# New offsets on the sort keys that order the expert steps of an attention, mixture-of-experts and FFN kernel

## The chip, the cores and the metric

The kernel runs on one core of one Trainium2 chip. The metric is the device time of one execution in microseconds; the time of a kernel is the median of its runs. The core has five engines, each of which takes its instructions in the order in which they were written for it: TensorE (PE, matrix products; its weight loads are shown as PEld), VectorE (DVE), ScalarE (ACT), GpSimd (POOL) and SyncE (SP), which here only issues DMA transfers. ACT and POOL issue DMA transfers as well. Engines wait for each other by semaphores.

## The reference, cut to what matters

```python
attn_out = _attn_ref(q, k, v)            # 8 batches, 8 heads, 576 rows, 64 columns; linear attention
x = attn_out.transpose(0, 2, 1, 3).reshape(4608, 512)

logits = x @ w_gate                      # one of 8 experts for each token
e_idx = argmax(logits, axis=1)
gate_w = softmax(logits)[e_idx]
eom = 1.0 / (1.0 + exp(-(x @ w_output_gate)))
for e in range(8):
    mask = e_idx == e
    h = maximum(x[mask] @ w1[e], 0.0)    # 512 -> 1024
    out[mask] = gate_w[mask] * eom[mask, e] * (h @ w2[e])   # 1024 -> 512

h = out @ w_in                           # 512 -> 2048
return (h * cos(h)) @ w_out              # 2048 -> 512
```

All of it is float32, with 4608 tokens.

## The kernel before, in words

The kernel has three stages, which follow one another on PE: the attention with the gate (0 to 183 us of the span), the expert steps (183 to 661 us), and the FFN (its first products start at 669 us and run to the end).

A float32 product is made of three products in the fast matrix type: each operand is split into a high part and a remainder (`wh` and `wl` for weights, `xTh` and `xTl` for tokens, `hh` and `hl` for the hidden layer), and high by high, high by remainder and remainder by high are added in PSUM. The three products are L1141, L1143 and L1144 for the first expert layer (`mm1`, 128x256 outputs) and L1177 to L1179 for the second (`mm2`, 128x512 outputs).

**The expert steps.** After the tokens are sorted by expert, 22 steps j = 0 to 21 each take a block of tokens of one expert. Their kinds are D F D F D F H D F H F D F H D F H D F H F F: F is a step of 256 tokens (two tiles of 128), D is also one of 256 but shares its expert's weights with the step behind it, and H is a step of 128 tokens, one tile. The first two steps use tokens that are known early; those from j = 2 on need the sort. A step does this, for a tile a = 0, 1:

- POOL gathers the token rows by an indirect DMA (`gather`, L277) into one of two `xg` buffers and scales them (`norm`, L282); PE transposes them (`trans`, L287), ACT and DVE split them (`xhigh` L294, `xlow` L299). The names of these operations in the order are gat, norm, tr, xh and xl, and they are for a later step while the current one runs.
- SP loads a quarter of the expert's weights as they are (`wload`, L256, named ld; 1 MB each, three `raw` buffers); ACT rounds it in two halves (`whigh`, L264, named wh), DVE makes the remainder (`wlow`, L268, named wl). There is one set of wh/wl buffers for each of the four quarters, so a quarter is only split after the last product that reads the old one. Loads are numbered over the run: 4 for each change of expert weights.
- PE computes the first layer in four blocks n (named mm0 and mm1, the two halves of a block: a block has 24 products in an F or D step and 16 in an H step). In an H step the high and the remainder part of the tokens stand side by side, and ACT and DVE first add the two halves of the result (`hsum`, L1152/L1153, named hs). ACT takes the relu (`hhigh`, L1162, hh), DVE the remainder (`hlow`, L1166, hl). The block buffers in PSUM are three.
- PE computes the second layer (`mm2`); ACT copies the result out of PSUM (`yout`, L1183, named y) and issues its store on its own DMA queue (L1185).

**The sort** (operations named s: cnt, px, base, pos, hot, low, mm_0 to mm_2, inv, exp, eI, more, far, gate, done) runs beside steps 0 and 1. `mm_0` to `mm_2` are 36 small products of PE (L978); `inv` gives the row numbers that the gathers from step 2 on need.

**The conversion.** The FFN's weights come as 64-bit numbers. Beside the expert steps, 32 jobs load them (`c_load`, L1058, SP's queue, named cld; 'i' for the jobs of w_in, 'o' for those of w_out), and ACT, DVE and POOL turn them into float32 (csq L1063, clf L1066, ca L1071, ch L1075, cp L1079, cm L1082, cs L1086, cw L1099). Jobs 'o' store the result to memory from ACT's queue (chi, L1104). From the jobs 'i', sums and differences of blocks are made (wsum L1114 on POOL), split (whi L1122, wlo L1126) and stored (wst, L1129, ACT's queue), seven parts each time. Rows of the output that no token has are zeroed from ACT's queue too (zero, L1191).

At the end (Z operations): the first rows of the FFN's input are gathered (L1202), scaled (L1205), transposed (L1210) and copied (L1216), summed and split (xs L844, oh L852, ol L857).

**What sets the order.** Each operation is registered by `op(key, name, fn, *deps)`: `key` is a due time in a plan in which an F step is 21.6 long, a D step 21.4 and an H step 12.06 (L1190 to L1230 hold the tables). The plan's step starts are 43.6 for j = 2, 65 for j = 3 and 129.6 for j = 6. The table `SHIFT` (L1418 to L1451) adds an offset to the key, for each kind of operation and place; the place (`place`, from L1453 on) is for instance the kind of step (D, F, H, or the number for j = 0 to 2) and the tile, block or quarter. For gat, norm, tr, xh and xl, and for ld, wh and wl, the kind is that of the step before the one that they are for. Then `issue` (L24 to L56) writes the operations out: of all whose dependencies are written, always the one with the smallest key. An offset changes only the order; the operations, their engines and their buffers stay.

Of the kernel before, what the change touches and what calls it, by code (L numbers as in the profile page):

```python
# [56 lines left out]
def kernel(  # L57
# [14 lines left out]
    B, H, S, D = q.shape  # L72
# [38 lines left out]
    xs = dram.tile([N, XW], F32, name="xs")  # L111
# [125 lines left out]
    wh, wl, rawt, ereg = {}, {}, {}, [None]  # L237
# [64 lines left out]
    with ExitStack() as actx:  # L302
# [386 lines left out]
        for b in range(B):  # L689
# [45 lines left out]
            for c in range(C):  # L735
                i = C * b + c
# [7 lines left out]
            if b % 2:  # L744
                i = NM + b // 2
# [113 lines left out]
    with bctx:  # L859
# [229 lines left out]
        wf, wsum, wst = {}, {}, {}  # L1089
# [324 lines left out]
        for i, (at, e1, e2) in enumerate(ZO):  # L1414
# [4 lines left out]
            chi={('o',): 12.7},  # L1419
            cld={('i',): -3.65, ('o',): -18.9},  # L1420
            cm={('i',): 11.5, ('o',): 10.7},
            cp={('o',): 3.4},
            csq={('i',): 1.55, ('o',): 1.9},
            cw={('i',): 3.15, ('o',): 7.6},
            gat={('2', 1): 10.85, ('D', 0): -15.4, ('H', 1): 9.1},
            hh={('0', 2): 7.8, ('1', 2): -3, ('1', 3): -36.3, ('D', 0): 0.4, ('D', 1): 4.2, ('F', 2): -72.8, ('F', 3): -45.95,
                ('H', 3): -1.05},
            hl={('1', 1): 3.05, ('1', 3): -14.1, ('D', 2): 6.4, ('F', 2): -33.3, ('F', 3): -88.65, ('H', 3): -72.1},
# [3 lines left out]
            oh={(3,): 3.6, (4,): 25.85, (5,): 18.6},  # L1432
# [3 lines left out]
            wh={('1', 0, 0): -1.8, ('1', 2, 1): 5.25, ('F', 2, 0): -20.4, ('F', 2, 1): -0.95, ('F', 3, 0): 1.1, ('F', 3, 1):  # L1436
                0.85, ('H', 0, 0): -111.6, ('H', 0, 1): -36.8, ('H', 2, 0): -0.15, ('H', 2, 1): -3.4, ('w3', 0): -45.2, ('w3',
                1): -18.25},
            whi={(1,): 18.9, (2,): 17.9, (5,): 17.65},
            wl={('1', 0, 0): 4.65, ('1', 1, 0): 4.25, ('1', 2, 0): 3.35, ('F', 2, 1): 2.45, ('H', 0, 0): -164.95, ('H', 1, 0):  # L1440
# [321 lines left out]
```

## Time and profile before

| | us |
|---|---|
| median of three runs | 1454.03 |
| the three runs | 1454.03, 1456.35, 1449.67 |
| the profiled execution | 1452.48 |
| its span, first to last instruction | 1450.7 |
| mean granted clock of PE in it | 0.987 of full speed |

The span is what the profile's views divide up; the profiled execution's own time has the 1.8 us around it as well. A wait in a list of waits is idle time of the engine named first, up to the instruction given; the releaser is what ended it, inferred from semaphores. In a timeline, the idle time before an instruction stands in square brackets, and a line with xN stands for N neighbouring instructions. PEclk in a table of windows is the mean granted clock of PE, 1.00 being 2.4 GHz.

### The profile page before, as it was taken

The page shows a single profiled execution, that of the slowest core. Times are in us where ns is not written, and L with a number is a line of the kernel's source. Part 1 is how long each engine was busy: PE and PEld are TensorE (multiplying, and loading weights), DVE is VectorE, ACT ScalarE, POOL GpSimd, SP SyncE. Part 2 cuts the span into 40 slices and gives each one's busy share as a digit, 9 for nine tenths or more (in the row PEclk, how much of TensorE's full clock was granted, in tenths as well). Part 3 has the DMA queues.
Part 4 walks back from the last instruction along what each step waited for, and adds up shares of the span by engine and source line. Part 5 has one row for each costly group of instructions (what it writes and reads, how often), then busy time and mean ns, then how long its engine had stood idle before and what let it go on. Part 6 is the DMA issues. An engine that isn't in the chain of part 4 may idle for free.

```text
span 1450.7 us, 25366 instructions
## 1 busy us (share of the span) xinstructions
PE 1399.1 (96%) x9530; PEld 1247.3 (86%) x9530; DVE 970.9 (67%) x1465; ACT 871.9 (60%) x1613; POOL 545.9 (38%) x391
## 2 busy tenths in 40 slices
PE   6898899999999999998999999999999999999998
PEld 5777788898889889897889888898888898898987
DVE  7999986777877888876655655555565554655544
ACT  3876525546464746566766666666665666666654
POOL 5555325653536455425170513315041340603000
PEclk8999899999999999999999999999999999999999
DMA  9884434767896886996666665766667576665762
GB/s 312 274 266 157 173 103 169 269 234 260 286 356 223 284 268 239 342 334 240 189 203 195 203 199 172 226 175 205 197 181 224 167 209 197 197 203 169 206 178 82
DMA packets 189731, 317.99 MB, mean 219 GB/s; under 512 B 27744, under 2 KB 60000, under 8 KB 189600
## 3 DMA queue, kind: packets, MB, share of 16 engines
q1 hardware_dynamic: 153760, 253.54, 55.6%
q10 hardware_dynamic: 29840, 42.92, 8.0%
q0 software_dynamic: 6000, 19.83, 4.2%
q8 instruction: 78, 1.28, 0.4%
q14 instruction: 53, 0.43, 0.1%
HBM read 264.17 MB, written 52.05 MB: 218 GB/s over the span
## 4 chain that ended last, share of the span: by engine, by line
PE 78%; DVE 11%; DMA 4%; ACT 4%; issue 2%; POOL 0%; ACTq 0%; SPq 0%; DVEq 0%; POOLq 0%
PE acc L1629 8%; PE acc L1628 8%; PE acc L1627 8%; PE bank L1563 7%; PE bank L1565 7%; PE bank L1564 7%; PE hp L1141 5%; PE hp L1144 5%; PE hp L1143 4%; PE yps L1177 4%; PE yps L1178 4%; PE yps L1179 4%; DVE m L384 2%; DMA raw<-in_moe_w_dram 1%; PE xp L527 1%
## 5 line engine op out<-in xcount | busy, mean ns | idle before, releaser
L1563 PE MATMUL bank<-xo,wp 128*128 128x256 f32 x994 | 281.6, 283 | 1.4 <-ACT part L1577 0.6
L1564 PE MATMUL bank<-xo,wp 128*128 128x256 f32 x994 | 277.4, 279 | 0.9 <-DVE xo L857 0.9
L1565 PE MATMUL bank<-xo,wp 128*128 128x256 f32 x994 | 277.6, 279 | 0.0
L1606 DVE SCALAR_TENSOR_TENSOR n<-n,h 128x512 f32<-128x512 f32 x144 | 125.6, 872 | 171.0 <-ACT n L1603 171.0
L1627 PE MATMUL acc<-wh,ht 128*128 128x512 f32 x576 | 227.6, 395 | 0.4 <-ACT ht L1612 0.4
L1628 PE MATMUL acc<-wl,ht 128*128 128x512 f32 x576 | 227.5, 395 | 0.0
L1629 PE MATMUL acc<-wh,ht 128*128 128x512 f32 x576 | 227.0, 394 | 0.4 <-DVE ht L1616 0.4
L1563 PEld LDWEIGHTS bank<-xo,wp 128*128 128x128 f32 x994 | 186.9, 188 | 22.4 <-ACT part L1577 4.1
L1564 PEld LDWEIGHTS bank<-xo,wp 128*128 128x128 f32 x994 | 186.7, 188 | 17.3 <-DVE xo L857 1.1
L1141 PE MATMUL hp<-xTh,wh 128*128 128x256 f32 x704 | 193.7, 285 | 5.8 <-DVE ht L1166 5.3
L1144 PE MATMUL hp<-xTh,wl 128*128 128x256 f32 x704 | 192.1, 282 | 0.0
L1565 PEld LDWEIGHTS bank<-xo,wp 128*128 128x128 f32 x994 | 187.5, 189 | 0.0
L268 DVE TENSOR_TENSOR wl<-raw,wh 128x1024 fp32r<-128x1024 f32 x121 | 164.6, 1379 | 11.2 <-ACT wh L264 10.6
L857 POOL TENSOR_TENSOR xo<-x,xo 128x512 fp32r<-128x512 f32 x24 | 31.1, 1296 | 371.2 <-ACT xo L852 371.2
L1585 DVE TENSOR_TENSOR h<-bank,part 128x256 f32<-128x256 f32 x213 | 89.3, 421 | 110.9 <-PE bank L1565 109.8
L1143 PE MATMUL hp<-xTl,wh 128*128 128x256 f32 x544 | 152.8, 281 | 1.3 <-DVE xTl L299 1.3
L1592 ACT ACTIVATE n<-h 128x512 int32<-128x512 f32 x144 | 91.1, 633 | 101.7 <-DVE h L1585 98.1
L264 ACT CAST wh<-raw 128x1024 fp32r<-128x1024 f32 x126 | 127.8, 1053 | 38.0 <-DMA raw<-in_moe_w_dram 18.5
L1141 PEld LDWEIGHTS hp<-xTh,wh 128*128 128x128 f32 x704 | 134.7, 191 | 7.0 <-DVE ht L1166 5.7
L1600 ACT ACTIVATE n<-n 128x512 f32<-128x512 f32 x144 | 91.1, 633 | 77.9 <-DVE n L1597 77.9
L1144 PEld LDWEIGHTS hp<-xTh,wl 128*128 128x128 f32 x704 | 134.7, 191 | 0.2
L1629 PEld LDWEIGHTS acc<-wh,ht 128*128 128x128 f32 x576 | 108.3, 188 | 26.8 <-DVE ht L1616 1.7
(310 smaller groups left out, 3083.4 us busy)
## 6 DMA issues: line engine op xcount, KB each, us to landing
wp<-ws SPq DMA_DIRECT2D x504, 256.0 KB, 2.8
raw<-in_moe_w_dram SPq DMA_DIRECT2D x60, 1024.0 KB, 7.9
ws<-wst ACTq DMA_DIRECT2D x28, 512.0 KB, 7.2
ys<-yt ACTq DMA_DIRECT2D x39, 256.0 KB, 5.9
xs<-xt ACTq DMA_DIRECT2D x36, 260.0 KB, 4.2
k<-in_k_dram SPq DMA_DIRECT2D x8, 1024.0 KB, 8.3
v<-in_v_dram SPq DMA_DIRECT2D x8, 1024.0 KB, 8.7
q<-in_q_dram SPq DMA_DIRECT2D x8, 1024.0 KB, 9.3
```

The lines of the kernel that those rows point to most:

```text
L264: sc.copy(out=wh[j, c][:, s], in_=rawt[c][:, s])
L268: eng.tensor_tensor(out=wl[j, c][:, s], in0=rawt[c][:, s], in1=wh[j, c][:, s], op=ALU.subtract)
L1141: pe.matmul(hp[:, f2, :], w_h, xTh[j][:, d, :], start=(d == 0), stop=False)
L1143: pe.matmul(hp[:, f2, :], w_h, xTl[j][:, d, :], start=False, stop=False)
L1144: pe.matmul(hp[:, f2, :], w_l, xTh[j][:, d, :], start=False, stop=(d == KD - 1))
L1563: pe.matmul(h, w[:, 0, k], x[:, i, 0, k], start=(first and k == 0), stop=False, skip_group_check=True)
L1564: pe.matmul(h, w[:, 0, k], x[:, i, 1, k], start=False, stop=False, skip_group_check=True)
L1565: pe.matmul(h, w[:, 1, k], x[:, i, 0, k], start=False, stop=(k == 1), skip_group_check=True)
L1606: ve.scalar_tensor_tensor(out=rs[j, s], in0=rs[j, s], scalar=-0.5, in1=hs[j, s], op0=ALU.add, op1=ALU.mult)
L1627: pe.matmul(acc[t, a], gh[f][:, ts], w_h, start=(c == 0), stop=False)
L1628: pe.matmul(acc[t, a], gh[f][:, ts], w_l, start=False, stop=False)
L1629: pe.matmul(acc[t, a], gl[f][:, ts], w_h, start=False, stop=(c == KF - 1))
```

## The change

Only the table `SHIFT` is replaced. No operation is added, dropped or given to another engine. A place that the new table lacks has the offset 0. The change's own words are that the offsets come from a search that also counts the shared semaphores and the common bandwidth of the transfers. The diff, cut to the entries that are spoken of:

```diff
         SHIFT = dict(
-            cld={('i',): -3.65, ('o',): -18.9},
-            cm={('i',): 11.5, ('o',): 10.7},
-            gat={('2', 1): 10.85, ('D', 0): -15.4, ('H', 1): 9.1},
-            hs={('H', 0): -80.25, ('H', 1): -138.15, ('H', 2): -3.05, ('H', 3): -91.25},
-            ld={('F', 2): -13.65},
-            norm={('1', 0): -18.3, ('1', 1): 16.25, ('D', 0): -3.75, ('F', 0): -3.2, ('H', 0): 7.1},
-            s={('exp',): 14.15, ('gate',): 11.85, ('hot',): 15.45, ('mm_0',): 11.05, ('more',): 13.55, ('pos',): 16.35,
-                ('px',): 2},
-            tr={('D', 0): -68.85, ('F', 0): -1.55, ('H', 0): -100.5, ('H', 1): -76.35, ('Z', 2): 0.55},
...
-            wst={(0,): 33.95, (1,): 29.4, (2,): 22.8, (3,): 31.35, (5,): 29.6},
-            xs={(0,): 4.7, (3,): 3.85},
-            y={('0', 0): 7.35, ('1', 0): 10.15, ('D', 1): 12.45, ('F', 0): 1.5, ('F', 1): -47.1, ('H', 0): 11.6},
+            cld={('i',): -2.05, ('o',): 12.1},
+            cm={('i',): 13.2, ('o',): 14.1},
+            cs={('i',): -18},
+            gat={('1', 1): 9.15, ('2', 1): -17, ('H', 0): -23.3},
+            hs={('H', 0): -179.55, ('H', 1): -71.3, ('H', 2): -7.8, ('H', 3): -44.75},
+            ld={('F', 0): -5.65, ('F', 1): -6, ('H', 0): 7.95, ('H', 2): 15.25, ('H', 3): 18.1},
+            norm={('2', 0): -14.15, ('F', 0): 7.35, ('F', 1): 7.9, ('H', 0): 6.55, ('H', 1): 7.65},
+            s={('done',): 12.7, ('far',): -68.15, ('low',): 8.3, ('mm_0',): 13.75, ('more',): 0.95, ('pos',): 19.85, ('px',):
+                3.4},
+            tr={('1', 1): 1.85, ('2', 1): 0.55, ('D', 0): -3.5, ('F', 0): 3.95, ('H', 0): -51, ('H', 1): -114.7, ('Z', 2):
+                1.25},
...
+            wst={(0,): 14.85, (1,): 8.2, (2,): 11.45, (3,): 28.9, (4,): 41.55, (5,): 5.2, (6,): 10.35},
+            xs={(2,): 57.1},
+            y={('1', 0): 1.75, ('1', 1): 6.25, ('D', 0): 4.25, ('F', 1): 1.35, ('H', 0): 5.6},
```

The entries of chi, cp, csq, cw, hh, hl, oh, wh, whi, wl, wlo, wsum, xh, xl and zero are replaced too, and entries for ca, ch and ol come in.

## Rows read from the trace of the kernel before

**Rows 1.** The page, its span and the busy time of each engine.

```profile
span 1450.7 us, 25366 instructions
...
PE 1399.1 (96%) x9530; PEld 1247.3 (86%) x9530; DVE 970.9 (67%) x1465; ACT 871.9 (60%) x1613; POOL 545.9 (38%) x391
```

**Rows 2.** Windows by stage: us, busy by engine, PEclk, DMA share, GB/s.

```profile
183.00:661.00 478.00, 466.90 (x3071) 421.71 (x3071) 366.88 (x504) 259.29 (x399) 229.44 (x164) 0.99 0.74 261
661.00:690.00 29.00, 25.08 (x160) 21.42 (x161) 20.06 (x29) 18.07 (x37) 15.64 (x12) 1.00 0.64 218
```

**Rows 3.** Waits of PE, 183 to 690 us: us in total, times, longest.

```profile
PE hp L1141 <- DVE ht L1166: 5.3, 2, 3.0
PE t L287 <- POOL xg L282: 3.5, 3, 2.3
PE t L1210 <- POOL yg L1205: 1.5, 1, 1.5
PE hp L1143 <- DVE xTl L299: 1.3, 2, 1.0
```

**Rows 4.** Timeline of PE, at four of its waits: start, us, instruction, idle before.

```profile
231.56 0.66 PE L287 MATMUL t<-ident,xg 128*128 128x128 f32 x4 [0.67 <-POOL xg L282]
...
237.24 0.68 PE L287 MATMUL t<-ident,xg 128*128 128x128 f32 x4 [2.27 <-POOL xg L282]
...
339.60 0.38 PE L1141 MATMUL hp<-xTh,wh 128*128 128x256 f32 x1 [2.25 <-DVE ht L1166]
...
404.15 0.39 PE L1141 MATMUL hp<-xTh,wh 128*128 128x256 f32 x1 [3.01 <-DVE ht L1166]
```

**Rows 5.** Windows behind three waits, and two undisturbed first layers; columns as above.

```profile
237.30:241.00 3.70, 3.70 (x20) 3.70 (x21) 0.97 (x1) 0.00 (x0) 3.57 (x3) 0.56 0.00 0
339.60:343.00 3.40, 3.40 (x17) 3.40 (x18) 3.21 (x5) 2.32 (x5) 0.21 (x1) 0.58 1.04 372
404.20:408.00 3.80, 3.80 (x19) 3.61 (x20) 3.48 (x6) 2.95 (x6) 2.05 (x2) 0.60 0.96 337
308.20:319.30 11.10, 11.10 (x99) 11.05 (x99) 5.54 (x9) 4.04 (x6) 4.60 (x4) 1.00 0.70 260
349.10:360.50 11.40, 11.40 (x99) 11.40 (x98) 10.02 (x14) 7.83 (x13) 3.78 (x3) 1.00 0.27 94
```

**Rows 6.** Timeline of POOL from 218 us, and the tile xg from 217 to 236.

```profile
217.99 0.98 POOL L277 DMA_INDIRECT xg<-xs,invI  x1 [22.06 <-DVE es L1021]
220.60 1.31 POOL L1082 TENSOR_TENSOR rw<-rw,a 128x512 f32<-128x512 f32 x1 [1.62 <-ACT yt L1183]
...
223.81 2.13 POOL L282 TENSOR_TENSOR xg<-xg 128x512 f32<-128x512 f32 x1 [0.77 <-DMA xg<-xs,invI]
226.09 1.24 POOL L277 DMA_INDIRECT xg<-xs,invI  x1
...
236.09 1.10 POOL L282 TENSOR_TENSOR xg<-xg 128x512 f32<-128x512 f32 x1 [2.07 <-DMA xg<-xs,invI]
...
L287 PE MATMUL t<-ident,xg x8: 272/273/330, 227.5 to 231.9; 128*128 128x128 f32 x8
...
DMA to landing us min/median/max: 3.6/5.0/7.1
```

**Rows 7.** Timeline of PE, the products of the sort.

```profile
214.74 1.92 PE L978 MATMUL sp<-rpi,ht 128*128 128x108 bf16 x36
```

**Rows 8.** Timeline of ACT ahead of the H steps j = 6 and j = 9.

```profile
336.25 0.34 ACTq L1185 DMA_DIRECT2D ys<-yt  x1
336.63 0.37 ACT L1152 COPY ht<-hp 128x256 f32<-128x256 f32 x1 [5.07 <-DMA raw<-in_moe_w_dram]
...
397.14 0.59 ACT L1183 COPY yt<-yps 128x512 f32<-128x512 f32 x1 [5.40 <-DMA raw<-in_moe_w_dram]
```

**Rows 9.** Timeline of SP at 326 us, and how long that transfer took.

```profile
326.23 0.37 SPq L256 DMA_DIRECT2D raw<-in_moe_w_dram  x1
...
DMA to landing us min/median/max: 9.9/9.9/9.9
```

**Rows 10.** Waits of SP, 183 to 661 us: us in total, times, longest.

```profile
SPq L1058 <- DVE sq L1099: 65.9, 7, 15.2
```

More of the change, by code (lines that the diff above doesn't have):

```diff
@@ L1435 @@
-            tr={('D', 0): -68.85, ('F', 0): -1.55, ('H', 0): -100.5, ('H', 1): -76.35, ('Z', 2): 0.55},
[L1436 to L1440, printed above, removed]
-                -18, ('H', 1, 1): -7.45, ('H', 2, 0): -0.25, ('H', 3, 0): -1.25, ('w3', 0): -58.35},
@@ L1442 @@
[L1442 to L1449 removed]
+            ca={('o',): -6},
@@ new lines @@
+            ch={('o',): 5.4},
+            chi={('o',): 12.9},
+            cld={('i',): -2.05, ('o',): 12.1},
+            cm={('i',): 13.2, ('o',): 14.1},
+            cs={('i',): -18},
+            csq={('i',): 8.15},
+            cw={('i',): -24.4, ('o',): 10.55},
+            gat={('1', 1): 9.15, ('2', 1): -17, ('H', 0): -23.3},
+            hh={('D', 0): 7.35, ('D', 1): 3.75, ('D', 2): 7.8, ('D', 3): 5.75, ('F', 0): 2.7, ('F', 1): 2.65, ('F', 2): 2.5,
+                ('F', 3): -0.15, ('H', 0): 1.35},
@@ new lines @@
+            hl={('1', 0): 5.15, ('1', 1): 3.75},
+            hs={('H', 0): -179.55, ('H', 1): -71.3, ('H', 2): -7.8, ('H', 3): -44.75},
+            ld={('F', 0): -5.65, ('F', 1): -6, ('H', 0): 7.95, ('H', 2): 15.25, ('H', 3): 18.1},
+            norm={('2', 0): -14.15, ('F', 0): 7.35, ('F', 1): 7.9, ('H', 0): 6.55, ('H', 1): 7.65},
+            oh={(1,): 7.05, (3,): 6.45, (6,): 23.3},
+            ol={(4,): 29.45},
+            s={('done',): 12.7, ('far',): -68.15, ('low',): 8.3, ('mm_0',): 13.75, ('more',): 0.95, ('pos',): 19.85, ('px',):
+                3.4},
@@ new lines @@
+            tr={('1', 1): 1.85, ('2', 1): 0.55, ('D', 0): -3.5, ('F', 0): 3.95, ('H', 0): -51, ('H', 1): -114.7, ('Z', 2):
+                1.25},
+            wh={('1', 0, 0): -0.4, ('1', 1, 0): -14.2, ('1', 3, 0): 15.95, ('F', 0, 0): 2.6, ('F', 1, 0): 1.3, ('F', 2, 0):
+                -39, ('H', 0, 0): -22.4, ('H', 0, 1): -28.4, ('H', 1, 0): 4.6, ('w3', 0): -6.4},
+            whi={(1,): -3.2, (3,): 20.65, (5,): 5.5, (6,): -12.15},
+            wl={('1', 0, 0): -11.5, ('1', 0, 1): -10.8, ('1', 1, 0): -14, ('1', 1, 1): 14.7, ('1', 2, 1): 4.8, ('F', 3, 0):
+                -14.4, ('H', 0, 0): -54.55, ('H', 0, 1): 1.45, ('H', 1, 0): -11.6, ('H', 2, 1): 3.9},
@@ L1450 @@
+            wlo={(1,): -5.85},
+            wst={(0,): 14.85, (1,): 8.2, (2,): 11.45, (3,): 28.9, (4,): 41.55, (5,): 5.2, (6,): 10.35},
+            wsum={(1,): 14.55, (3,): 34.1},
+            xh={('2', 1): 2.85, ('D', 0): 7.6, ('H', 0): -1.35, ('H', 1): 3.7},
+            xl={('H', 0): -1.55},
+            xs={(2,): 57.1},
+            y={('1', 0): 1.75, ('1', 1): 6.25, ('D', 0): 4.25, ('F', 1): 1.35, ('H', 0): 5.6},
+            zero={(): 0.15},
         )
```

13 lines of the change are left out of this document (removed).

## The prediction

> **What bounds the kernel now.** The page's first two lines come first: TensorE (PE) is busy for 96% of a span of 1450.7 us [rows 1], so time can be saved only where PE stands idle or runs slowly. A table by stage says where that is inside the stretch whose order the change rewrites: the expert steps (183 to 661 us) leave PE idle for 478.00 - 466.90 = 11.1 us and the start of the FFN for 29.00 - 25.08 = 3.9 us [rows 2]. These 15.0 us, and what the clock costs, are all that an order can win.
>
> Next, what PE waits for there. In the list of PE's waits the largest entries are the first-layer products of the half-size steps waiting for the remainder `ht` of the step before (5.3 us in two waits) and the transposes waiting for the gathered rows `xg` (3.5 us in three) [rows 3]. The timeline puts them at 237.24 us (2.27 us, a transpose), 339.60 (2.25) and 404.15 (3.01), the last two in the H steps j = 6 and j = 9 [rows 4]. Behind each of the three the granted clock is lower: 0.56 for 3.7 us, 0.58 for 3.4 us, 0.60 for 3.8 us, where undisturbed stretches show 1.00 (2.4 GHz against 1.2 GHz for a part of the stretch) [rows 5]. So each wait is paid twice.
>
> **Wait 1, the gathers.** POOL issues the gather of tile (2,0) at 217.99 us, waits for it, normalizes, and only then, at 226.09, issues that of (2,1); a transpose frees the buffer for (3,0), whose rows are normalized from 236.09 on [rows 6]. The transpose of (3,0) stands ahead of step 2's first product on PE, so PE waits for it at 237.24. Price: 2.27 us, another 0.67 us at the transpose of (2,1) [rows 4], and 3.7 x (1 - 0.56) = 1.63 us of clock: **4.6 us**.
>
> The change issues (2,1) straight behind (2,0) and puts the transposes of (3,0) behind the third block of step 2, some 8 us later (three blocks of 24 products, by a step's 99 matmuls in 11.10 us [rows 5]). The wait at 237.24 has no cause left. Against that, `pos` and `mm_0` go back, so the sort's 36 products on PE (1.92 us from 214.74 on [rows 7]) go behind one more block of 24, 2.7 us by the same row. The gathers, which wait for the sort, start 2.7 us later: at 220.7 and, one issue of 1.24 us on, 221.9. With the first one's landing (217.99 to 223.81: 5.8 us) its rows come at 226.5 and are normalized, in 2.13 us, by 228.6; PE was ready for their transposes at 227.5 [rows 6], so it is 1.1 us late. Then POOL has two operations of the conversion (1.31 us for the one shown, taken twice) and the second normalization: 228.6 + 2.6 + 2.1 = 233.3, where PE, ready at 231.56 - 0.67 [rows 4] and now 1.1 later, waits from 232.0: 1.3 us. Residual **2.4 us**. Bounds: with the shortest landing shown, 3.6 us, the first is in time and the second 0.2 late; with the longest, 7.1, 1.3 us more, 3.7. I take the value between, since it is this gather's own. No clock is charged: a lower one stands in [rows 5] only behind the three waits over 2 us of [rows 4].
>
> **Waits 2 and 3, the H steps.** At 336.25 ScalarE (ACT) issues the output store of y(5,1), and the copy that starts the H step's first sum stands behind it; it was held 5.07 us, and the releaser named is the landing of a raw weight load [rows 8]. Nothing that a store needs is a weight load, but the load issued on SP's queue at 326.23 took 9.9 us [rows 9], which ends at 336.1, just ahead of the store. I read this as a completion semaphore that the two transfers share: the later issue waits for the earlier landing. The same ahead of 397.14: the copy that follows the store of a combined weight block shows 5.40 us of waiting for a raw load [rows 8]. Price: 2.25 + 3.4 x 0.42 = 3.7 us, and 3.01 + 3.8 x 0.40 = 4.5 us.
>
> The change moves y('F',1) from -47.1 to +1.35: behind the H step's first sum instead of ahead of it. What stood behind the held store now stands ahead of it; a store that is held there holds the copy of y, which the step needs only when its PSUM buffer comes round, three tiles on. The weight stores are issued earlier or later (wst 1 from 29.4 to 8.2, wst 3 hardly), and the conversion's loads `cld 'o'` 31 us later, so that three of them no longer follow on the raw load of [rows 9]. Both waits go in the forecast: **8.2 us**. Bounds: all, or nothing if the next store in turn is held just as long.
>
> A rule stands against this part. The Trainium skill, "DMA: Bandwidth & Descriptors", section "Issuing engines are not separate DMA queues", has all queues run on the same 16 DMA engines and interleave; by it an order on one queue does not take the other queue's bytes out of a load's way, and the gain of the loads would be nothing. The trace agrees as far as it goes: a raw load lands after 9.9 us. By the rule alone the sum would keep waits 2 and 3 and come to the 0.2 us of the rival *given back*, below.
>
> I take the store's position, not the load's time, for the gain, and so the 8.2 us.
>
> **The other moves.** 199 places on ACT, 125 on VectorE (DVE), 51 on POOL, 41 on PE and 25 of 91 on SP change. Nothing is added, so their instructions cost nothing by themselves; their cover is PE's 97.7% busy share in [rows 2], and what it costs if the cover is gone are new short waits. The transposes of other steps move from before the second layer to inside it, with less lead for the x copies; wh and wl of the sort's stretch come later; the raw buffers of loads 12 and 20 come free earlier, since the two halves of wl now stand side by side on DVE (credited with nothing, since SP's loads wait in both). I take one short wait at each of three places (sort, transposes, tail) at the size of the small ones now: 1.3 us in two [rows 3], so 3 x 0.65 = **2.0 us**; bounds 0 and, with the 1.5 us wait of L1210 [rows 3] at each, 4.5.
>
> **Sum.** 4.6 + 8.2 - 2.4 - 2.0 = 8.4 us. The profiled execution took 1452.48 us, its span 1450.7, the rest 1.8 lies around it; 1452.5 - 8.4 = 1444.1. The median of the runs shown, 1454.03, is 1.5 us above that execution, which puts the forecast at **1445.6 us**. One unknown remains that no row explains: a step's 99 matmuls took 11.10 us at 308.2 and 11.40 at 349.1 with the clock at 1.00 in both [rows 5]. If the new order moves a dozen steps from the one to the other, that is 12 x 0.3 = 3.6 us either way.
>
> **Rivals.** *Given back.* The shared semaphores remain, every ACT store takes a turn among the loads, and a new order makes other pairs. If the held stores are met again ahead of an H step's first sum (or ahead of the weights' casts on ACT), waits 2 and 3 move and do not go; then 4.6 - 2.4 - 2.0 = 0.2 us is won: about 1454. For it: which pair meets cannot be read from the offsets, and loads here take 9.9 us. Against it: the y store that headed the H step is gone from there in four of five cases, by its own key. The rule of the Trainium skill's page named above ("DMA: Bandwidth & Descriptors") would lead here too.
>
> *Slower: SP's queue is blocked.* SP issues in order. In the new order the loads cld 14 and 15 (and cld 30 and 31 near the end) stand ahead of the raw loads 22 (and 50). Such a `cld` waits until DVE has finished an earlier conversion, now up to 15.2 us [rows 10]; each us of it goes to the raw load behind, whose weights an H or F step casts as soon as the products before have read the buffers. It decides if load 22 is issued over 7 us into its step: the cast is due some 17 us in, and a landing takes up to 9.9. Then H steps stall at the worst price seen, 3.01 + 1.52 = 4.5 us; if all five do, three more than now, 3 x 4.5 = 13.6 us: about 1467. For it: those waits of SP are long. Against it: the conversions' stores and sums are earlier as well, and 31 us of delay puts most `cld` later than their buffers come free.
>
> **How the numbers follow.** Half a per cent is 7.3 us, about what a measurement here tells from no change; faster means below 1446.8. Forecast: 0.54, of which 0.13 falls short of that line, since 1445.6 is close to it. Given back: 0.28 (0.21 the same, 0.04 slower, 0.03 faster, by the unexplained pace). Blocked: 0.18, slower. Faster 0.41 + 0.03 = 0.44, same 0.13 + 0.21 = 0.34, slower 0.18 + 0.04 = 0.22. The range: at the low end all idle time and all clock losses of the stretch go, 15.0 + 4.6 = 19.6 us below the median, 1434.4; I cut it at 1436, since some waits of [rows 3] lie where nothing moves. At the high end one and a half H waits more than now, 6.8 us, give 1461; the full blocked case lies beyond. The forecast's own range: 1438 (residual 0.2, no new waits, 3.6 of pace) to 1449 (residual 3.7, new waits 4.5).
>
> **What would show it.** Right: no wait over 1 us by a transpose near 237 us, gathers of (2,0) and (2,1) one issue apart, no hs copy of an H step behind a store held by a raw load, the granted clock at 1.00 in j = 2, 6 and 9, PE idle for about 7 us in the expert steps (11.1 now, less the 8.2 of [rows 4], plus 4.4). Wrong: a wait of 2 us or more at the first product of any H step, the clock below 0.7 behind it, or SP's wait on a conversion ahead of raw loads 22 or 50 with casts waiting for the landing. If PE's idle time falls by 9 us and the total does not, the pace of the products is what gave it back.

## The result, and the profile after

| | before | after |
|---|---|---|
| median, us | 1453.15 (4 runs) | 1436.56 (4 runs, 1433.97 to 1438.03) |
| ratio of the runs, 95% interval | | 0.989 (0.9871 to 0.9909) |
| span of the profiled execution | 1450.7 | 1436.2 |
| first expert product to first FFN product | 485.8 (183.0 to 668.8) | 467.8 (187.2 to 655.0) |

The changed kernel is faster by 16.6 us. The prediction said 8.4 us (1445.6) with a range of 1436 to 1461: the direction was right, the time lies 0.6 us inside the range's low end, and the gain is twice the forecast's. A second set of runs on another chip gave 0.9872 (0.9838 to 0.9906).

The stretch from the first expert product to the first FFN product, called the stage below, is the cleanest measure: the order is rewritten in it (and for the FFN's first input, at its end), and it lost 18.0 us. The attention ahead of it, which has the same code in every kernel here, ended anywhere between 182.8 and 189.4 us in the profiles of this study, and that alone moves a total by up to 6.6 us, nearly what the forecast was worth. (In this pair it took 4.2 us more after the change; the FFN took 0.7 less; 18.0 - 4.2 + 0.7 = 14.5, the difference of the spans.)

The table of windows over the stage, first of the kernel before, then of the one after (with the first stretch of [rows 2], the three places where [rows 5] showed a low clock, and the stage's start):

```profile
183.00:668.80 485.80, 473.63 (x3104) 427.15 (x3105) 373.59 (x511) 261.44 (x402) 231.22 (x165) 0.99 0.73 257
```

```profile
183.00:661.00 478.00, 475.94 (x3177) 431.08 (x3175) 386.68 (x533) 269.45 (x418) 231.43 (x168) 1.00 0.77 265
187.20:655.00 467.80, 467.21 (x3104) 423.31 (x3104) 377.58 (x514) 263.31 (x405) 226.38 (x165) 1.00 0.78 267
239.50:250.80 11.30, 11.30 (x101) 11.27 (x100) 8.06 (x12) 6.39 (x11) 6.17 (x5) 1.00 0.91 303
331.80:340.00 8.20, 8.20 (x73) 8.18 (x72) 6.85 (x10) 5.95 (x10) 3.91 (x3) 1.00 0.83 243
391.80:400.00 8.20, 8.20 (x73) 8.17 (x72) 5.43 (x8) 6.05 (x10) 2.91 (x3) 1.00 0.96 329
187.20:192.40 5.20, 4.61 (x24) 4.39 (x24) 1.06 (x4) 0.00 (x0) 2.15 (x3) 0.67 0.34 106
```

The same 3104 products run in both. PE's idle time fell from 485.80 - 473.63 = 12.2 us to 467.80 - 467.21 = 0.6 us: 11.6 of the 18.0 us. Its busy time fell by the other 6.4 us; the three low-clock stretches, at 1.00 now in j = 2, 6 and 9, are worth 4.6 of that. Against them stands a low clock at the start of this profile's stage (0.67 for 5.2 us, 1.7 us), which e12, another profile of the same kernel, does not have (1.00 there). That leaves 3.5 us. About 1.1 of it is pace: first-layer products start 0.1134 or 0.1178 us apart, and 815 were of the second kind instead of 1068. The other 2.4 us of busy time were not taken apart.

What PE still waits for (same stretch as [rows 3]): of the four lines there only the last is left, with 0.6 us. The first line here is the attention's end; the line on `bank` is one of the FFN's first products.

```profile
PE sp L902 <- DVE ht L568: 0.8, 1, 0.8
PE bank L1567 <- DVE xo L857: 0.6, 1, 0.6
PE hp L1143 <- DVE xTl L299: 0.6, 1, 0.6
```

The gathers, on the timeline of POOL (answering to [rows 6]) and of PE (to [rows 7] and [rows 4]):

```profile
226.31 0.98 POOL L277 DMA_INDIRECT xg<-xs,invI  x1 [18.95 <-DMA ys<-yt]
227.60 0.95 POOL L277 DMA_INDIRECT xg<-xs,invI  x1 [0.30 <-issue]
230.90 1.04 POOL L282 TENSOR_TENSOR xg<-xg 128x512 f32<-128x512 f32 x1 [2.36 <-DMA xg<-xs,invI]
...
234.29 1.04 POOL L282 TENSOR_TENSOR xg<-xg 128x512 f32<-128x512 f32 x1
...
223.06 1.92 PE L978 MATMUL sp<-rpi,ht 128*128 128x108 bf16 x36
...
233.12 0.60 PE L287 MATMUL t<-ident,xg 128*128 128x128 f32 x4
236.32 0.60 PE L287 MATMUL t<-ident,xg 128*128 128x128 f32 x4
```

Both gathers are issued one issue apart, as read from the keys, and neither transpose has a bracket: PE did not wait. The H step j = 6 on ACT, answering to [rows 8]:

```profile
333.92 0.36 ACT L1152 COPY ht<-hp 128x256 f32<-128x256 f32 x1
334.18 0.59 ACT L1183 COPY yt<-yps 128x512 f32<-128x512 f32 x1
334.80 0.33 ACTq L1185 DMA_DIRECT2D ys<-yt  x1
```

The first sum stands ahead of the copy of y(5,1), and the store is issued right behind that copy. It is not held.

### The profile page after: what moved, and what is told of

Same layout as the page of the kernel before. It is cut to its first block, busy times and chain, and to the rows that moved or that the text cites. A ratio compares the mean times of both kernels' runs of the same rounds, so it can differ in the third digit from the quotient of the medians.

```text
span 1436.2 us, 25362 instructions
## 1 busy us (share of the span) xinstructions
PE 1393.4 (97%) x9530; PEld 1243.1 (87%) x9530; DVE 976.2 (68%) x1465; ACT 872.2 (61%) x1613; POOL 542.4 (38%) x391
## 4 chain that ended last, share of the span: by engine, by line
PE 83%; DVE 11%; ACT 3%; issue 2%; DMA 1%; SPq 0%; DVEq 0%; ACTq 0%
PE acc L1632 8%; PE acc L1630 8%; PE acc L1631 8%; PE bank L1566 8%; PE bank L1568 7%; PE bank L1567 7%; PE hp L1144 6%; PE hp L1141 6%; PE yps L1179 5%; PE yps L1178 5%; PE yps L1177 5%; PE hp L1143 4%; DVE m L384 2%; DVE n L1600 1%; DVE lt L549 1%
## 5 line engine op out<-in xcount | busy, mean ns | idle before, releaser
L1141 PE MATMUL hp<-xTh,wh 128*128 128x256 f32 x704 | 191.3, 282 | 0.0
L268 DVE TENSOR_TENSOR wl<-raw,wh 128x1024 fp32r<-128x1024 f32 x121 | 175.8, 1483 | 13.8 <-ACT wh L264 13.2
L1141 PEld LDWEIGHTS hp<-xTh,wh 128*128 128x128 f32 x704 | 133.0, 189 | 1.0
```

Source lines behind the costliest of these rows:

```text
L268: eng.tensor_tensor(out=wl[j, c][:, s], in0=rawt[c][:, s], in1=wh[j, c][:, s], op=ALU.subtract)
L1141: pe.matmul(hp[:, f2, :], w_h, xTh[j][:, d, :], start=(d == 0), stop=False)
```

## The experiments

Three theories of the H waits are told apart. *Position* (the prediction's): what costs is that a y store stands ahead of the H step's first sum on ACT. *Semaphore*: what costs is that the store shares its completion semaphore with a raw load in flight. *Transfer*: the loads are late among the conversion's loads. An overview first; idle is PE's, within the stage, from a table of windows over each; the ratio is to the kernel before, with its interval (e13 to e16 were run once and are judged by the stage alone).

| kernel | stage | idle | ratio |
|---|---|---|---|
| before | 485.8 | 12.2 | 1 |
| e1 one turn of the semaphores | 485.7 | 14.6 | 1.0006 (0.9979 to 1.0034) |
| e2 y('F',1) alone | 480.0 | 9.4 | 0.9989 (0.9964 to 1.0014) |
| e3 front alone | 526.9 | 42.1 | 1.0275 (1.0229 to 1.0322) |
| e4 tail alone | 485.3 | 12.5 | 1.0 (0.9979 to 1.0022) |
| e5 all of y | 483.7 | 12.5 | 0.9976 (0.9957 to 0.9995) |
| e6 three gather moves | 483.1 | 12.6 | 0.9963 (0.9928 to 0.9998) |
| e7 y and gather moves | 473.1 | 4.9 | 0.9929 (0.989 to 0.9969) |
| e8 change, old y | 475.2 | 6.8 | 0.9963 (0.9944 to 0.9983) |
| e9 change, old gathers | 471.4 | 4.6 | 0.9893 (0.9853 to 0.9934) |
| e10 conversion alone | 506.7 | 31.2 | 1.0139 (1.0088 to 1.0189) |
| e11 change, old conversion | 496.6 | 22.4 | 1.0107 (1.0072 to 1.0142) |
| e12 change again | 466.5 | 0.4 | 0.9872 (0.9838 to 0.9906) |
| e13 e7 and transposes | 484.6 | 13.4 | |
| e14 change, old splits | 497.6 | 21.3 | |
| e15 change, old tail | 467.3 | 1.5 | |
| e16 y, front, conversion | 497.9 | 21.3 | |

### e1 and e2: what holds the store, and what that costs

```diff
+        def pass_turn():
+            sy.dma_start(out=ys[128 * NH:128 * NH + 128, 0:128], in_=cv["zt"])
+
         def yout(j, a, slot):
+            if (j, a) == (5, 1):
+                pass_turn()
             t = P["yp"].tile([128, DM], F32, tag="yt", name="yt")
```

> The kernel before with one small store (64 KB of zeroes to rows that are zeroed anyway) put on SP's queue between the raw load ahead of the H step j = 6 and the store of y(5,1). Each transfer of SP and ACT takes the next of eight completion semaphores, so every later transfer moves on by one turn, and y(5,1) no longer shares the semaphore of that raw load. The order of all other work is that of before. Turn theory (a store is held because its completion semaphore is the one of a raw load in flight): the store of y(5,1) is issued up to 3.4 us earlier, the wait of 2.25 us at the first-layer products of j = 6 and the low clock behind it go, -3.7 us; the wait in j = 9 (3.01 us) stays, since its two transfers move on together. Position theory (the prediction's: what counts is that the y store stands ahead of the H step's first sum on ACT): no change, 0. Transfer theory (the raw load is late because of the conversion's loads around it, and everything waits for the load): 0.

In the program as built, each transfer of SP and ACT takes the next of eight semaphores, and one that takes a semaphore waits for the transfer that had it. The records of the traces name the semaphore of each transfer and bear the pairs out: SP's and ACT's use eight numbers; in the kernel before, the raw load of [rows 9] and y(5,1) both have 107, and the store held until 396.71, ahead of j = 9, has 109 with the raw load that landed at 396.69. With one transfer put between, y(5,1) has 109 with a weight store that landed at 336.14. The timelines of ACT and PE in e1 show that exchange and its effect, at j = 6, 9 and 16:

```profile
336.22 0.34 ACTq L1190 DMA_DIRECT2D ys<-yt  x1
336.60 0.37 ACT L1152 COPY ht<-hp 128x256 f32<-128x256 f32 x1 [1.69 <-DMA ws<-wst]
...
405.50 0.58 PE L1141 MATMUL hp<-xTh,wh 128*128 128x256 f32 x1 [2.96 <-DVE ht L1166]
...
550.38 0.37 ACT L1152 COPY ht<-hp 128x256 f32<-128x256 f32 x1 [4.41 <-DMA raw<-in_moe_w_dram]
...
553.35 0.38 PE L1141 MATMUL hp<-xTh,wh 128*128 128x256 f32 x1 [1.65 <-DVE ht L1166]
```

The copy at j = 16 in the kernel before:

```profile
546.54 0.37 ACT L1152 COPY ht<-hp 128x256 f32<-128x256 f32 x1 [2.80 <-DMA raw<-in_moe_w_dram]
```

The releaser is the weight store now, the copy behind waits 1.69 us instead of 5.07 [rows 8], and the wait at j = 6 is gone, while that of j = 9 stands at 2.96 (3.01 before), as the semaphore theory said. It is not chance: in e4 and e6, where y(5,1) keeps its semaphore and its place, the copy waits 4.38 and 4.46 us, and PE waits 1.63 and 1.64 us at j = 6. But the stage did not get shorter. At j = 16 the copy behind a y store now waits 4.41 us for a raw load instead of 2.80, and PE waits there for 1.65 us, where it had not waited at all. What was won at j = 6 was in part lost at j = 16, as the prediction's rival *given back* has it; that the turn did this is not shown, since e6, with the order of stores of before, has 4.45 and 1.64 us there too. A wait of a transpose at 499 us grew as well, from 0.52 to 1.64 us. The eight holds at j = 6 and 16 before and in e1, e4 and e6 line up: behind 1.69, 2.60 and 2.80 us PE did not wait, behind 4.38 to 4.46 it waited 1.63 to 1.65, behind 5.07 it waited 2.25: the hold less about 2.8 us. Here a hold cost PE only what went beyond the work that PE still had.

```diff
-            y={('0', 0): 7.35, ('1', 0): 10.15, ('D', 1): 12.45, ('F', 0): 1.5, ('F', 1): -47.1, ('H', 0): 11.6},
+            y={('0', 0): 7.35, ('1', 0): 10.15, ('D', 1): 12.45, ('F', 0): 1.5, ('F', 1): 1.35, ('H', 0): 11.6},
```

> The kernel before with one entry of the new table, y('F',1) from -47.1 to +1.35: the second y store of an F step stands behind the first sum of the H step that follows. The completion semaphores keep their pairs (the store of y(5,1) still shares that of the raw load). Position theory (the prediction's): the waits at j = 6 and j = 9 go, -8.2 us, or -3.7 if only j = 6. Turn theory: the store is held as long as before, and now the relu of the H step's first block stands behind it, which the products of the fourth block need just as much: the wait at j = 6 stays at about 2 us, total 0 (within 2 us).

The timeline of ACT at j = 6, and the largest waits of PE in 183 to 690 us:

```profile
335.34 0.60 ACT L1183 COPY yt<-yps 128x512 f32<-128x512 f32 x1
336.77 0.34 ACTq L1185 DMA_DIRECT2D ys<-yt  x1
337.15 0.37 ACT L1152 COPY ht<-hp 128x256 f32<-128x256 f32 x1 [1.21 <-DMA raw<-in_moe_w_dram]
```

```profile
PE t L287 <- POOL xg L282: 2.8, 2, 2.3
PE hp L1143 <- DVE xTl L299: 2.4, 3, 1.1
```

The store still waits for the raw load, now 1.21 us, with work done ahead of it; and no line "hp L1141 <- DVE ht" is left at all. Both H waits are gone, j = 9 included, and the stage lost 5.8 us; new waits of about 1 us took the rest of the 8.2 expected. So both theories hold a half: the shared semaphore is why a store is held, and its place on ACT is why that costs PE anything. Taking away either one removed the wait at j = 6; only the new place shortened the stage. (That the j = 9 wait hangs on its store's semaphore too is read from the trace; no run here changed that pair alone.) (The ratio of the totals, 0.9964 to 1.0014, leaves at most 5.2 us of it: it does not resolve so little, and the stage is one profiled execution.)

### e3, e4: the front and the tail alone

e3 takes the entries s, gat, norm, tr, xh and xl of the new table (the diff of the change has most of them), e4 the entries of the tail:

```diff
-            oh={(3,): 3.6, (4,): 25.85, (5,): 18.6},
-            xs={(0,): 4.7, (3,): 3.85},
+            oh={(1,): 7.05, (3,): 6.45, (6,): 23.3},
+            ol={(4,): 29.45},
+            xs={(2,): 57.1},
```

> The kernel before with the new offsets of the sort, the gathers, the norms, the transposes and the splits of the tokens (s, gat, norm, tr, xh, xl) alone. By the prediction's first part: the waits of the transposes at 231.6 and 237.2 us and the low clock behind the second go, -4.6 us, with a residual of 0 to 2.4. Turn theory: this order moves one conversion load ahead of the store of the weight block that was held until 396.7, which thereby gets another semaphore; the wait in j = 9 goes too, another -4.5 us, while the wait at j = 6 stays, since its pair of transfers keeps one semaphore: -9 us together. Position theory: y('F',1) and the weight stores keep their offsets, so both H waits stay: -2 to -4.6 us.

```profile
PE hp L1141 <- ACT xTh L294: 19.8, 5, 5.2
```

Every expected stage missed: 41 us longer. The waits of transposes for gathers are gone from the list, but the splits of the tokens (`xTh`) now stand on ACT behind casts of weights, which wait for raw loads (at 662 us two such casts, after 2.71 us of waiting, run straight ahead of the split), and five steps wait 2.9 to 5.2 us each. The new front does not stand alone.

> The kernel before with the new offsets of the sums and splits of the FFN's first input (xs, oh, ol) alone. The prediction charged new short waits at the tail and credited none; in the changed kernel the idle time of TensorE from 653 us (before) to the first FFN products and in the 20 us behind them fell by about 3 us. If these offsets did it: -1 to -3 us. If those waits hang on the transfers and the last steps instead (the gather of the FFN's first rows comes after the stores of y): 0.

485.3 against 485.8, ratio 1.0: the tail's offsets do nothing in the old order. This makes e4 a second look at the kernel before up to the tail, and a measure of scatter: its waits are 3.40 us at the transpose of (3,0), 1.63 at j = 6 and 1.59 at j = 9, where [rows 4] has 2.27, 2.25 and 3.01. These three waits moved by 0.6 to 1.4 us between the two executions, their sum (6.6 and 7.5) and the stage by less than 1.

### e5 to e7: the two parts of the forecast, alone and together

e5 takes the whole entry y of the new table. e6 takes three moves, the transposes for the one tile alone:

```diff
-            y={('0', 0): 7.35, ('1', 0): 10.15, ('D', 1): 12.45, ('F', 0): 1.5, ('F', 1): -47.1, ('H', 0): 11.6},
+            y={('1', 0): 1.75, ('1', 1): 6.25, ('D', 0): 4.25, ('F', 1): 1.35, ('H', 0): 5.6},
```

```diff
-            gat={('2', 1): 10.85, ('D', 0): -15.4, ('H', 1): 9.1},
+            gat={('2', 1): -17, ('D', 0): -15.4, ('H', 1): 9.1},
...
             norm={
+                ('2', 0): -14.15,
...
             tr={
+                ('3', 0): -3.5,
...
             if t in ("gat", "norm", "tr", "xh", "xl"):
+                if n == ("tr", 3, 0):
+                    return ("3", 0)
```

> The kernel before with the whole new entry y. Beside y('F',1) (tried alone: the expert stage, from the first expert product to the first FFN product, went from 485.8 to 480.0 us) it brings y('H',0) from 11.6 to 5.6, so the store of the last H step, j = 19, which the gathers of the FFN's first rows wait for, stands earlier on ACT. Position theory: the stage loses another 2.1 us (the waits of 1.49 and 0.64 at the transposes of L1210) and what follows from them at 670.9 us: 477 to 478. Rival (the tail's waits come from the offsets of the conversion and the loads): the L1210 wait stays at 1.5 us, stage 480.

```profile
PE t L287 <- POOL xg L282: 5.0, 2, 3.4
PE hp L1141 <- DVE hx L1166: 1.8, 1, 1.8
```

The tail's wait at L1210 is gone, so the H step's earlier store is what the tail had waited for. No wait for `ht` stands at j = 6 or j = 9. But the stage was 483.7, longer than e2's: the transpose of (3,0) waited 3.40 us (as in e4; 2.26 in e2), and 1.8 us went at the first steps, which the entry's offsets for the steps 0 and 1 move too. The expectation was missed by 6 us, and which of these is the entry's own is not settled.

> The kernel before with three moves alone: the gather of tile (2,1) straight behind that of (2,0), the norm of (2,0) ahead of the conversion on POOL, and the transposes of the one tile (3,0) behind the third block of step 2. The sort stays where it was. By the prediction's first part, without the later sort: the waits of 0.67 and 2.27 us at the transposes and the low clock behind them (1.63 us) go, the stage is 4.6 us shorter: 481.2 us. Rival (the rows come late whatever the order on POOL, since a gather lands after 3.6 to 7.1 us): the wait at the transposes of (2,1) or (3,0) stays over 1 us, the stage is within 2 us of 485.8.

```profile
PE hp L1141 <- DVE ht L1166: 5.9, 5, 1.6
PE t L1210 <- POOL yg L1205: 1.7, 1, 1.7
```

The waits at the transposes of (2,1) and (3,0) are gone, with no residual. The H waits stay: 1.64 at j = 6, 1.58 at j = 9 and, new, 1.64 at j = 16, and the stage came to 483.1, not 481.2.

> The kernel before with the new entry y and the three moves of the gathers together. If the gains are separate and add up: stage 485.8 - 8 - 4.6 = 473 us, against 467.8 of the whole change; the difference of 5 us is left for all other entries (about 500 moved places). If one takes the other's place (a wait covered by the other): 477 or more.

```profile
PE t L287 <- POOL xg L282: 1.9, 3, 0.7
PE hp L1143 <- DVE xTl L299: 1.4, 2, 1.1
```

473.1 us where 473 was expected: together the two parts give 12.7 us, more than they give apart (2.1 and 2.7). No wait over 1.1 us is left. This is what the forecast's sum was about: 4.6 + 8.2 = 12.8. Apart, each left the other's waits standing and met waits of 1 to 1.8 us in other steps; why those are missing when both are in was not settled.

### e8, e9: the same parts undone in the changed kernel

e8 is the changed kernel with the old entry y (the diff of e5 the other way), e9 with the offsets of the three moves set back:

```diff
-            gat={('1', 1): 9.15, ('2', 1): -17, ('H', 0): -23.3},
+            gat={('1', 1): 9.15, ('2', 1): 10.85, ('H', 0): -23.3},
...
             norm={
-                ('2', 0): -14.15,
...
             tr={
+                ('3', 0): -68.85,
```

> The changed kernel with the old entry y. The store of y(5,1) shares its semaphore with a store of zeroes issued long before and is not held. If a store's place on ACT costs only where it is held by a load in flight (both theories together): no wait of 2 us at j = 6 or 9; the last H step's store is late again, so the tail's wait of about 1.5 to 2 us at L1210 comes back: stage 469 to 470 us. If the place alone costs, whatever the semaphore: the two H waits of 2 to 3 us come back, stage 474 to 478.

```profile
PE yps L1179 <- DVE ht L1166: 3.3, 2, 1.7
PE hp L1141 <- DVE ht L1166: 1.7, 1, 1.7
PE t L1210 <- POOL yg L1205: 1.5, 1, 1.5
```

No wait of 2 us at j = 6 or 9 came back, and the tail's wait did: as expected of both theories together (no copy of an H step's sum was held here). But the stage rose by 7.4 us, 5 more than that, through waits of 1.6 to 1.7 us at 388, 441 and 595 us that neither theory named. An early copy of y moves the work of ACT behind it, which may be the cause, but no run shows it.

> The changed kernel with the three moves of the gathers undone: the gather of (2,1) behind the norm of (2,0) and the conversion on POOL, and the transposes of (3,0) ahead of step 2's first product. If the first part of the prediction is right: the waits of the transposes come back, at (3,0) 2 to 3.5 us with about 1.6 us of clock behind it, stage 467.8 + 4 to 6 = 472 to 474 us. Rival (the rest of the new order covers it): stage within 1.5 us of 467.8.

The wait on PE's timeline, the gather of the same rows on POOL's, and the window behind the wait (236 to 240 us):

```profile
236.01 1.12 PE L287 MATMUL t<-ident,xg 128*128 128x128 f32 x4 [4.26 <-POOL xg L282]
...
227.23 1.04 POOL L282 TENSOR_TENSOR xg<-xg 128x512 f32<-128x512 f32 x1
228.42 1.25 POOL L277 DMA_INDIRECT xg<-xs,invI  x1
234.92 1.04 POOL L282 TENSOR_TENSOR xg<-xg 128x512 f32<-128x512 f32 x1 [5.25 <-DMA xg<-xs,invI]
```

```profile
236.00:240.00 4.00, 3.99 (x14) 3.34 (x15) 2.16 (x3) 2.32 (x4) 2.27 (x3) 0.62 0.45 135
```

471.4 against 466.5 to 467.8: one wait of 4.26 us, with the clock at 0.62 for 4 us behind it; the stage is 0.6 us below the expected range. But the wait is not at (3,0). It is at the transposes of (2,1), whose gather is issued only behind the norm of (2,0) again and whose rows come 6.5 us after that. The third move was not undone: with the offset -68.85 the transposes of (3,0) stand behind the first block of step 2 here (at 243.49), not ahead of its first product, and do not wait. So the gather's place is shown from both sides (e6 and e9); that the transposes of (3,0) had to move is shown from the side of e6 alone, together with the other two moves.

### e10 to e16: the other entries

e10 takes the entries cld to chi, wsum, whi, wlo, wst, zero and ld of the new table into the kernel before, e11 those of the old table into the changed kernel. e13 is e7 with two entries more:

```diff
-            tr={('D', 0): -68.85, ('F', 0): -1.55,
+            tr={('D', 0): -3.5, ('F', 0): 3.95,
```

e14 and e15 are the changed kernel with the old entries wh, wl, hh, hl, hs, and with the old xs, oh, ol; e16 is the kernel before with the new y, front and conversion.

> The kernel before with the new offsets of the conversion, the raw loads, the weight and zero stores alone (cld to chi, wsum, whi, wlo, wst, zero, ld). The y stores and the gathers keep their places. In this order the store of y(5,1) and the tenth weight store take the semaphores of stores of zeroes, not of raw loads in flight. Semaphore and transfer theory: the stores ahead of the H steps j = 6 and j = 9 are not held, both H waits go, -8.2 us: stage 477 to 479; the transposes' waits near 237 us stay. Position theory alone: the y stores still head the H steps on ACT, waits of 2 to 3 us at j = 6 and j = 9 stay, stage 484 to 487.

ACT ahead of j = 6, and PE's wait there:

```profile
340.04 0.62 ACT L1122 CAST wst<-wsum 128x512 fp32r<-128x512 f32 x1 [6.72 <-POOL wsum L1114]
...
342.22 0.33 ACTq L1185 DMA_DIRECT2D ys<-yt  x1
...
345.61 0.38 PE L1141 MATMUL hp<-xTh,wh 128*128 128x256 f32 x1 [1.62 <-DVE ht L1166]
```

Neither theory gave 506.7: the transposes waited 16.4 us in seven places. The store of y(5,1) was not held (its copy ends at 342.19 and it is issued at 342.22), which the semaphore theory had right, but PE waited 1.62 us at j = 6 all the same: ACT had stood 6.72 us ahead of the cast of a combined weight block, which waited for POOL, with both copies of y and the H step's first sum behind it. So here it was another wait ahead of that sum on ACT that cost; a held store is one case of it. The conversion's new offsets need the rest as much as the front's do.

> The changed kernel with the old offsets of the conversion, the raw loads, the weight and zero stores. Here the tenth weight store shares the semaphore of a raw load in flight again, and the store of y(5,1) that of an older raw load. Since y stands behind the H step's first sum, by the position theory nothing of 2 us comes back at j = 6 or 9: stage 468 to 473 (the y and gather moves with the old conversion gave 473.1). Semaphore and transfer theory alone: a wait of 2 to 3 us with its clock comes back at j = 9, stage 472 to 476. The rival of the prediction that went to the slower side (SP blocked by conversion loads that stand ahead of raw loads) would make the old conversion the faster one: under 467.

ACT ahead of j = 7, and PE's wait there:

```profile
347.30 1.04 ACT L264 CAST wh<-raw 128x1024 fp32r<-128x1024 f32 x1 [5.37 <-DMA raw<-in_moe_w_dram]
...
348.25 0.58 ACT L294 CAST xTh<-t 128x512 fp32r<-128x512 f32 x1
...
348.88 0.58 PE L1141 MATMUL hp<-xTh,wh 128*128 128x256 f32 x1 [4.93 <-ACT xTh L294]
```

496.6, outside all three expected ranges. The raw load lands late (it was issued at 335.56 and took 11.7 us, where the stage's median is 7.7), the cast of `wh` stands on ACT and waits for it, and the split of the tokens stands behind the cast; the same happens at 417 us, with 6.34 us. No H wait of 2 us came back, as the position theory said. This has the end of the prediction's slower rival (a late raw load, casts that wait), in the old order of the loads and not in the new one, but not its cause: SP did not stand at a conversion load ahead of these two raw loads. In the changed kernel ACT's casts wait 8.4 us for raw loads in the whole stage, before 18.5.

> The changed kernel once more, to see how far its stages repeat: expert stage within 1.5 us of 467.8 (the kernel before and two kernels near it gave 485.8, 485.7 and 485.3), no wait over 1 us in it. The attention ahead of it, which no kernel here changes, ended anywhere from 182.8 to 189.4 us in the profiles so far, so the total is uncertain by that. A theory by which the pace of the products or the clock gave the gain, not the waits, would have another profile of it differ by several us in the stage.

466.5, idle 0.4: the stage repeats within 1.3 us, and the three kernels with the old order (before, e1, e4) within 0.5.

> The kernel before with the new entry y, the three moves of the gathers, and the new places of the first transposes behind every D step (-3.5 for -68.85) and every F step (3.95 for -1.55). In the run without these two (stage 473.1) the transposes of other steps still waited 0.71, 0.41, 0.51 and 0.70 us and a first-layer product 1.06 for xTl. If the places of the transposes cause the last 6 us: stage 470 to 471, these waits gone. If the transposes need the rest of the order (as the front offsets alone did, which cost 41 us): waits for xTh of 1 us and more, stage 475 or longer.

484.6: six waits of transposes for their rows, 11.4 us, and not the waits for xTh that the rival named. The places of the transposes alone are not what is missing in e7; without the rest they cost 11.5 us.

> The changed kernel with the old offsets of the weights' splits and of the hidden layer (wh, wl, hh, hl, hs). If these offsets are needed with the new places of the transposes and conversion: waits for xTh, ht or wl of 1 to 6 us, as with the old conversion, stage over 475. If they only follow: within 3 us of 467.

```profile
PE hp L1143 <- DVE xTl L299: 8.7, 11, 1.9
PE sp L962 <- DVE fl L960: 6.4, 1, 6.4
PE yps L1179 <- DVE ht L1166: 3.7, 2, 1.9
```

497.6: the offsets of wh, wl, hh, hl and hs are needed. The largest part of the 21.3 us of idle time is DVE's split of the tokens (`xTl`), late eleven times; one wait in the sort is the next.

> The changed kernel with the old offsets of the tail (xs, oh, ol). In the old order the new tail changed nothing (485.3 against 485.8). If the tail's gain comes from the earlier store of the last H step alone: stage within 1.5 us of 467, and the FFN's first 20 us wait for xo or part by 0 to 2 us more.

467.3: the tail's offsets are not needed in the stage; the waits in the FFN's first 20 us sum to 4.0 us, where the changed kernel's two profiles have 1.7 and 3.3.

> The kernel before with the new offsets of y, of the front (sort, gathers, norms, transposes, splits of the tokens) and of the conversion and loads together; weights' splits, hidden layer and tail as before. If front and conversion each fail alone only for want of the other: stage 467 to 471. If the weights' splits are needed too: waits of 1 us and more for xTh or ht, stage over 475.

497.9, with the same three waits as e14 (8.7, 6.4 and 3.8 us). The two kernels differ only in the tail's offsets, so this is e14 once more, within 0.3 us: the weights' splits are needed. Front alone (e3), conversion alone (e10), and the change without the new conversion (e11) or the new splits (e14) are all slower than either whole order; the new conversion and splits with the whole old front were not tried. The conversion or the splits alone at their old values cost 29 to 30 us (e11, e14); with the front at its old values as well, but for the three gather moves, the whole costs about 6 (e7 against the change).

## Why the prediction was half as large as the gain

The steps that failed are terms of the sum. Two charges were made for waits that did not come (a residual of 2.4 us at the gathers and 2.0 us of new short waits; the change has neither), and the small waits outside the three parts, 4.0 us, were held in place without a reason; 3.4 us of them went.

- **What bounds the kernel.** Right: the gain is mostly idle time of PE and the clock behind it, in the stretch named, and nearly all of that: 0.6 us of idle time is left of 12.2, where the prediction looked for about 7.
- **"So each wait is paid twice."** Right for the three waits priced, but not for waits of that size as such. The same wait of 2.26 us at (3,0) had a clock of 1.00 behind it in e1 and a low one in the kernel before; e3 has 2.87 us with 1.00 behind, e14 1.77 us with 0.64. A wait's clock is a price that may or may not come.
- **Wait 1, the gathers (4.6 us).** The waits went as forecast (e6), and e9 shows the gather's place from the other side. The residual of 2.4 us was wrong; it was 0. The gathers started 39.1 us into the stage (226.31), before 35.0: 4.1 us later, where 2.7 was forecast; but PE came to the transposes 1.4 us later as well (45.9 for 44.5), so against PE the forecast was right. (In e12, without the low clock at the start, the gathers start 2.6 us later and PE comes at 44.4.) What failed is that two durations were taken over. The first rows' wait ended after 230.90 - 226.31 = 4.6 us, not 5.8, and the normalization took 1.04 us, not 2.13 [rows 6]; e12 has 4.7 and 1.04. The 2.13 belonged to DVE's work beside it (last section). The landing may belong to the traffic: the DMA share was 0.79 from 218 to 224 us before, and 0.53 from 226.3 to 231 after; no run changed that alone.
- **Waits 2 and 3 (8.2 us).** The reading was right: the shared semaphore holds the store (e1), and its place on ACT makes it cost (e2, and e8, where the old place without a hold brings no H wait back). The size held only together with the gathers: e2 gave 5.8, and e7, y with the gathers, 12.7 of the 12.8 us of both parts.
- **The new short waits (2.0 us charged).** This is the term furthest off. The sum kept all waits below 2 us where they were, and added three of 0.65 us. The change took the old ones away and added none: of the 12.2 us of idle time only 8.2 stood in the three parts, and 3.4 of the other 4.0 went too. With these 3.4, the 4.4 of residual and charge, and the 1.8 us by which busy time fell beyond the three clock stretches, 8.4 becomes 18.0, the stage's loss. So about two thirds of the gain (12.7 us, e7) have a cause that the runs show. The tail's small wait is part of them (y('H',0), e5 and e8). The other 5.3 us came with front, conversion and splits together, and which offset ends which of those small waits stays open.
- **The rivals.** *Given back* did not come in the change: the stores meet other semaphores, and no hold stands ahead of an H step's sum. In e1 something like it came: the wait at j = 6 went and one at j = 16 appeared. Loads still land slowly (a raw load's median in the stage went from 8.0 to 7.1 us), and the gain came all the same; the rule of the Trainium skill on shared DMA engines, which the prediction set beside this rival, was not tested by any run. *Slower* did not come in the change; late raw loads with casts that wait came in e11, without SP standing at a conversion load.
- **The chances.** Faster by over half a per cent had 0.44, the largest of the three, and came; the range's low end, 1436, was cut above the 1434.4 at which all idle and clock losses go. That case, all idle time gone, is nearly the one that came, and it had no chance of its own in the forecast.

## What to carry to other kernels

Where an order is searched as a whole, cost it as a whole: take the idle time of the stretch as the gain's upper end and give that end a real chance. Here the search removed the small waits together with the large ones, and one part of its result without the others cost 41 us. A transfer's issue is an instruction in its engine's order like any other; look in the timeline for an issue that directly follows the landing of an unrelated transfer, and put work that PE needs ahead of it. Measure such a change by the stage that it touches, between two landmarks, where the total moves by several us on its own.

## What the runs showed of the hardware that was not expected

POOL's normalization of one tile took 2.13 us before and 1.04 us after. What differs is DVE. The timelines of DVE, before and after:

```profile
223.82 1.21 DVE L268 TENSOR_TENSOR wl<-raw,wh 128x1024 fp32r<-128x1024 f32 x1
224.95 1.53 DVE L1099 SCALAR_TENSOR_TENSOR wf<-sq,rw 128x512 f32<-128x512 f32 x1
```

```profile
230.06 1.28 DVE L1166 SCALAR_TENSOR_TENSOR hx<-hp,hx 128x512 fp32r<-128x512 f32 x2
234.37 1.51 DVE L1099 SCALAR_TENSOR_TENSOR wf<-sq,rw 128x512 f32<-128x512 f32 x1 [3.03 <-POOL rw L1086]
```

These are two ends of one spread: the 39 normalizations take 1.04 to 2.13 us in both kernels. Before, POOL's operation is shown from 223.81 to 225.94: beside it DVE's remainder of the weights takes its usual 1.21 us, and DVE's next operation, which takes 0.68 us elsewhere, is shown with 1.53 and ends about 0.5 us after POOL. After, DVE reads PSUM for one of its inputs (`hp`) and then stands idle, and POOL takes 1.04. At 234.29 it is the other way round: POOL starts first and takes 1.04, and DVE's operation of 0.68 us is shown with 1.51. That fits the two engines taking turns where both read SBUF and DVE reads two tensors of it. The Trainium skill, "SBUF — State Buffer", section "Who interferes with whom", says so: "A DVE instruction with two SBUF inputs contends with a GpSimd instruction that reads SBUF". The trace agrees: 2.13 us is 1.04 plus 1.09, about the 1.2 us that DVE's operation had to run. No run here set out to test it.

The pace of first-layer products has two values at the same clock, 0.1134 and 0.1178 us from start to start, and it can change within a step behind transposes (in the changed kernel from the second to the first at 354 us). Every kernel here shows both, in other steps each time. What chooses it stays open; over the stage it came to 4.8 us above the faster value in the kernel before and 3.6 in the one after, too little to carry the gain.
